# The gates of the last four chunks as one batch over 128 partitions

## The chip, the cores and the metric

The kernel runs on one core of a Trainium2 chip. The metric is the time of one execution on the device in microseconds (us), as the median of several runs. The engines are TensorE (PE: matmuls; PEld: loading of weights), VectorE (DVE), ScalarE (ACT), GpSimd (POOL) and SyncE (SP, which here only issues DMAs). Each works through its own queue in order.

## The reference

Two layers follow each other: a recurrent attention (mLSTM) with 4 batches, 8 heads, 768 steps and heads of 40, and a gated feed-forward layer on its output.

```python
for t in range(S):                                   # S = 768
    m_new = np.maximum(f_gate[:, :, t] + m, i_gate[:, :, t])
    f_stab = np.exp(f_gate[:, :, t] + m - m_new)
    i_stab = np.exp(i_gate[:, :, t] - m_new)
    m = m_new
    C = f_stab * C + i_stab * outer(vt, kt)          # per batch and head, 40 x 40
    n = f_stab * n + i_stab * kt
    y[:, :, t] = sigmoid(o_gate) * (C @ qt) / max(|n . qt|, 1)
# x: y with batch and step as rows (3072), head and channel as columns (320)
out = (sigmoid(x @ w_gate) * (x @ w_val)) @ w_out    # 320 -> 1536 -> 320
```

The change concerns only the running maximum `m` and the running sum of `f_gate`: two gates for each of 32 pairs (batch, head) and 768 steps.

## The kernel before

The steps are cut into 6 chunks of L = 128. A unit (c, b) is one chunk of one batch. Within a chunk the recurrence becomes matrix products: scores of q and k, times a matrix `d` of decay weights; between chunks a state `cst` is carried, scaled by `cdec`. The feed-forward layer works on chunk c for all four batches at once (512 columns), in 12 slices j of the 1536 hidden columns: `ffn_up` (L532 to L544) makes the two products into `pg0` and `pg1`, then `sg`, and its high and low parts `gh` and `gl`; `ffn_down` (L554 to L556) adds slice j into four banks `po`. The first four slices of chunk 0 are done in halves of 256 columns. Weights come as 64-bit numbers and are decoded piece by piece (`w_dec`: L259 on ScalarE, L264, L265, L269 on VectorE, L294 to L299 on ScalarE, L304 to L310 on POOL) between these slices.

The stages of a unit: `st_a` transposes q and k (L357) and copies them (L359, L361) and masks q (L362); `dmat` turns the loaded `d` tile into weights (L226 on ScalarE, mask L235 on POOL); `st_b` makes the scores (L426) and weights them (L427); `st_c` sums the values (L452), and with it the state is updated (`st_e`, L500 to L517) and the next unit's operands are prefetched (L135 to L138, `dmat_load` L219); `st_d` transposes the result into `xh` and `xl` (L488 to L491).

The gates. `f_gate` and `i_gate` are loaded as 32 rows (batch, head) by 768 steps into the tile `gin`, which holds the first slot of the tag "xh"; the running maxima lie in `mg`, the first slot of the tag "xl". Both slots are used again by `st_d` of chunk 1. Chunk 0 has its gates at the start (`gates_first`), chunk 1 in the opening (operation "gc"), chunks 2 to 5 in `gates_of(2, NCH)`: one running sum over 512 columns, which a tile `rst` of ones and zeros restarts at each chunk, one subtraction, then for each chunk a running maximum that starts at the end value `mend` of the chunk before, and the new end value; at last one subtraction of all maxima from the end values. Each chunk's maxima go to a scratch tensor `mscr[c]` in HBM, from which `dmat_load` reads them back, one row broadcast to all 128 partitions. `gate_transpose` (L195) turns sums and decays by TensorE, one transpose per chunk, into `at` (copied by VectorE, L197) and `dec` (exponential on ScalarE, L199), 128 steps by (chunk, batch, head); `gates_turn` derives `cdec` by a matmul (L207) and three VectorE operations (L208, L213).

The order outside the opening is a list of events by position, in units of a feed-forward slice, from a table `pos`, with clamps that keep it possible. A slice is emitted at its start, its `ffn_down` 0.46 later than the start of the slice behind it. The events g1, h1 and k1 stand for chunks 2 to 5's gates, `at` and `dec` with `cdec`; their positions are 0.599, 5.3 and 5.5. Position 4.0 is the first slice of 512 columns (its first matmul ends up on the queue at 76.6 us). The framework then makes each engine's queue from the emitted instructions by priority and its own model of what is ready when; `issue_after(x)` keeps instructions behind `x` on `x`'s engine.

Of the kernel before, what the change touches and what calls it, by code (L numbers as in the profile page):

```python
# [74 lines left out]
def mlstm_then_gated_ffn_kernel(  # L75
# [71 lines left out]
    mend = const.tile([BH, NCH + 1], F32, name="mend")  # L147
# [20 lines left out]
    def gate_max(c):  # L168
        cs = slice(c * L, (c + 1) * L)
        mc = m0[:BH] if c == 0 else mg[:, cs]  # L170
        nc.vector.tensor_tensor_scan(mc, ag[:, cs], ag[:, cs], mend[:, c : c + 1], ALU.max, ALU.max)
        nc.vector.tensor_tensor(mend[:, c + 1 : c + 2], fc[:, cs][:, L - 1 : L], mc[:, L - 1 : L], ALU.add)
        nc.sync.dma_start(mscr[c], mc)

    def gates_first():
        cs = slice(0, L)
        nc.vector.tensor_tensor_scan(fc[:, cs], ones, fg[:, cs], 0.0, ALU.mult, ALU.add)
        nc.vector.tensor_tensor(ag[:, cs], ig[:, cs], fc[:, cs], ALU.subtract)
        gate_max(0)


    def gates_of(c0, c1):
        cs = slice(c0 * L, c1 * L)
        nc.vector.tensor_tensor_scan(fc[:, cs], rst[:, cs.start - L : cs.stop - L], fg[:, cs], 0.0, ALU.mult, ALU.add)
        nc.vector.tensor_tensor(ag[:, cs], ig[:, cs], fc[:, cs], ALU.subtract)
        for c in range(c0, c1):
            gate_max(c)
        before = mend[:, c0:c1].unsqueeze(2).broadcast_to([BH, c1 - c0, L])
        nc.vector.tensor_tensor(dmx[:, cs].rearrange("p (c l) -> p c l", l=L), before,
                                mg[:, cs].rearrange("p (c l) -> p c l", l=L), ALU.subtract)  # L190

    def gate_transpose(src, dst, c0, c1, func):
        pt = ps_a.tile([P, c1 - c0, BH], F32, tag="pa", name=f"ptg{c0}_{c1}")
        for c in range(c0, c1):
            nc.tensor.transpose(pt[:, c - c0, :], src[:, c * L : (c + 1) * L], ident[:BH, :BH])  # L195
        if func is None:
            nc.vector.tensor_copy(dst[:, c0:c1, :], pt)  # L197
        else:
            nc.scalar.activation(dst[:, c0:c1, :], pt, func)  # L199
# [4 lines left out]
    def gates_turn(c0, c1):  # L204
        gate_transpose(dmx, dec, c0, c1, AF.Exp)
        pt = ps_a.tile([P, c1 - c0, B, H], F32, tag="pa", name=f"pt_cdec{c0}")
        nc.tensor.matmul(pt, sel, dec[:, c0:c1, :], start=True, stop=True)  # L207
# [8 lines left out]

    def dmat_load(c, b):
        d = dm_tile(c, b)
        nc.sync.dma_start(d, mscr[c][b * H : (b + 1) * H, :].partition_broadcast(P))  # L219
# [303 lines left out]
    def ffn_up(c, j, t0, t1):  # L523
# [20 lines left out]
        E('gl0' if c == 0 else 'gl').tensor_tensor(gl[u][:, :nt], sg, gh[u][:, :nt].bitcast(F32), ALU.subtract)  # L544
        return last
# [28 lines left out]
    def opening():  # L574
# [3 lines left out]
        nc.sync.dma_start(fg, f_gate.rearrange("b h s -> (b h) s"))  # L578
        nc.scalar.dma_start(ig, i_gate.rearrange("b h s -> (b h) s"))
# [28 lines left out]
        nc.gpsimd.memset(rst, 1.0)  # L608
        nc.gpsimd.memset(rst.rearrange("p (c l) -> p c l", l=L)[:, :, 0:1], 0.0)
# [333 lines left out]
```

## Time and profile before

| | |
|---|---|
| runs (median; lowest to highest of 3) | 572.35 us; 571.94 to 572.92 |
| span of the profiled execution | 569.9 us; the median of the runs is 2.45 us above it, and no separate time was kept for this execution |
| PE, PEld | 546.7 us (96%), 497.0 us (87%) |
| DVE, ACT, POOL | 319.5 us (56%), 232.2 us (41%), 162.2 us (28%) |
| DMA | 72.27 MB, mean 127 GB/s |

The profile is one execution. Times in it start at 0 with the span. The page gives for each engine the busy share in 40 slices of 14.25 us, and the chain of work that ended last; the timeline gives the single instructions, with start, duration, engine, line, output and inputs, and in brackets the time that the engine stood idle before it and what ended this. "ACT L299 ... [2.13 <-DVE dc L269]" reads: ScalarE idled 2.13 us before this instruction until VectorE's line 269, which writes dc, was done.

### The profile page before, as it was taken

To read this page: it belongs to the slowest core of one execution; us is meant where nothing else is said; L and a number is where in the kernel's file an instruction comes from. 1 tells how busy PE (TensorE), PEld (TensorE's weight loads), DVE (VectorE), ACT (ScalarE), POOL (GpSimd) and SP (SyncE) were. 2 spreads that over 40 slices of the span, in tenths; PEclk is the share of its full clock that TensorE was granted. 3 is DMA by queue.
4 is the path that set the end of the run, shared out by engine and by line. 5 is a ranking of instruction groups with operands and counts; after the bars stand their busy time and mean duration, and the time that the engine had idled before them with its cause. 6 is when DMAs were issued, how large, how long until landed. Compare 5 with 4: busy or idle time off the path is not lost.

```text
span 569.9 us, 9906 instructions
## 1 busy us (share of the span) xinstructions
PE 546.7 (96%) x3587; PEld 497.0 (87%) x3587; DVE 319.5 (56%) x739; ACT 232.2 (41%) x581; POOL 162.2 (28%) x231
## 2 busy tenths in 40 slices
PE   8667999999999999999999999999999999999997
PEld 7565988788899999998888888888888888999996
DVE  5788878895755645555555544545543545432322
ACT  5285657754443442352243241433342332232322
POOL 5567646575420241311322310332210210000000
PEclk9789999999999999999999999999999999999999
DMA  9797747242674947354666544685644824010000
GB/s 197 193 240 185 202 123 192 93 115 54 169 173 119 183 103 182 100 147 125 167 125 156 132 141 129 149 171 124 140 125 134 206 56 121 4 47 2 24 2 23
DMA packets 131641, 72.27 MB, mean 127 GB/s; under 512 B 103113, under 2 KB 120777, under 8 KB 131593
## 3 DMA queue, kind: packets, MB, share of 16 engines
q1 hardware_dynamic: 130504, 71.39, 50.6%
q8 instruction: 28, 0.46, 0.3%
q10 hardware_dynamic: 1088, 0.26, 0.2%
q14 instruction: 21, 0.16, 0.1%
HBM read 56.95 MB, written 14.68 MB: 126 GB/s over the span
## 4 chain that ended last, share of the span: by engine, by line
PE 85%; DVE 7%; ACT 3%; issue 2%; POOL 2%; POOLq 0%; DVEq 0%; ACTq 0%
PE pg L532 34%; PE po L554 7%; PE po L556 7%; PE po L555 7%; PE av L452 6%; PE pg L534 6%; PE pg L537 6%; PE in L447 2%; PE s L434 2%; PE pt L373 2%; PE xt L488 2%; PE cs L500 2%; PE s L426 1%; DVE dc L264 1%; ACT d L226 1%
## 5 line engine op out<-in xcount | busy, mean ns | idle before, releaser
L539 ACT ACTIVATE sg<-pg 128x256 f32<-128x256 f32 (+1 forms) x103 | 48.3, 469 | 174.3 <-PE pg L537 174.2
L540 DVE SCALAR_TENSOR_TENSOR sg<-sg,pg 128x256 f32<-128x256 f32 (+1 forms) x103 | 53.9, 524 | 113.9 <-ACT sg L539 110.6
L532 PE MATMUL pg<-xh,wl 128*128 128x256 f32 (+1 forms) x412 | 111.1, 342 | 1.2 <-POOL wl L304 1.2
L532 PE MATMUL pg<-xh,wh 128*128 128x256 f32 (+1 forms) x412 | 110.9, 343 | 0.4 <-DVE sg L540 0.4
L532 PE MATMUL pg<-xl,wh 128*128 128x256 f32 (+1 forms) x412 | 108.7, 339 | 0.0
L556 PE MATMUL po<-oh,gl 128*128 128x320 f32 x288 | 93.0, 323 | 0.0
L554 PE MATMUL po<-oh,gh 128*128 128x320 f32 x288 | 92.3, 321 | 0.4 <-ACT gh L543 0.4
L555 PE MATMUL po<-ol,gh 128*128 128x320 f32 x288 | 92.4, 321 | 0.0
L544 DVE TENSOR_TENSOR gl<-sg,gh 128x256 fp32r<-128x256 f32 (+1 forms) x103 | 59.6, 579 | 35.5 <-ACT gh L543 34.9
L532 PEld LDWEIGHTS pg<-xh,wl 128*128 128x128 f32 x412 | 70.9, 191 | 8.5 <-POOL wl L304 1.4
L532 PEld LDWEIGHTS pg<-xh,wh 128*128 128x128 f32 x412 | 70.9, 191 | 5.8 <-DVE sg L540 0.6
L532 PEld LDWEIGHTS pg<-xl,wh 128*128 128x128 f32 x412 | 69.3, 190 | 6.6
L543 ACT ACTIVATE gh<-sg 128x256 fp32r<-128x256 f32 (+1 forms) x103 | 51.7, 502 | 47.7 <-DVE sg L540 47.7
L554 PEld LDWEIGHTS po<-oh,gh 128*128 128x128 f32 x288 | 54.5, 189 | 2.0 <-ACT gh L543 0.6
L555 PEld LDWEIGHTS po<-ol,gh 128*128 128x128 f32 x288 | 54.4, 189 | 1.3
L556 PEld LDWEIGHTS po<-oh,gl 128*128 128x128 f32 x288 | 54.2, 188 | 0.5 <-DVE gl L544 0.2
L534 PE MATMUL pg<-xh,w 128*128 128x256 f32 (+1 forms) x206 | 52.9, 332 | 0.7 <-POOL v L139 0.4
L537 PE MATMUL pg<-xl,w 128*128 128x256 f32 (+1 forms) x206 | 53.1, 331 | 0.0
L452 PEld LDWEIGHTS av<-v,d 128*128 128x128 f32 x352 | 46.8, 191 | 2.2 <-DVE d L427 0.6
L452 PE MATMUL av<-v,d 128*128 128x41 f32 x352 | 45.5, 269 | 0.4 <-DVE d L427 0.3
L508 POOL TENSOR_TENSOR cst<-cst,cdec 120x246 f32<-120x246 f32 (+1 forms) x32 | 16.0, 519 | 98.9 <-PE in L447 98.9
L235 POOL TENSOR_SCALAR_AFFINE_SELECT d<-d 128x1024 f32<-128x1024 f32 x22 | 24.2, 1101 | 50.1 <-ACT d L230 46.0
(128 smaller groups left out, 834.5 us busy)
## 6 DMA issues: line engine op xcount, KB each, us to landing
d<-mscr SPq DMA_DIRECT2D x22, 512.0 KB
ks<-scr SPq DMA_DIRECT2D x16, 360.0 KB
qs<-scr SPq DMA_DIRECT2D x16, 360.0 KB
k<-in_k_dram SPq DMA_DIRECT2D x24, 160.0 KB
v<-in_v_dram SPq DMA_DIRECT2D x24, 160.0 KB
o<-in_o_gate_dram SPq DMA_DIRECT2D x24, 160.0 KB
st_o<-in_moe_w_out_dram SPq DMA_DIRECT2D x12, 320.0 KB
out_dram<-ob SPq DMA_DIRECT2D x24, 160.0 KB
```

Source lines behind the costliest of these rows:

```text
L235: nc.gpsimd.affine_select(out=d, in_=d, pattern=[[0, H], [1, L]], compare_op=ALU.is_ge, fill=0.0, base=0, channel_multiplier=-1)
L452: nc.tensor.matmul(pv[:, h, :], dm[u][:, h, :], vt[u][:, h, :], start=True, stop=True)
L532: nc.tensor.matmul(pg[n], w[n][:, a, fs], x[c][:, a, n0:n1], start=(i + a == 0), stop=False)
L534: nc.tensor.matmul(pg[n], w2[n][:, fs], xh[c][:, 2, n0:n1], start=False, stop=False)
L537: nc.tensor.matmul(pg[n], w2[n][:, fs], xl[c][:, 2, n0:n1], start=False, stop=True)
L539: nc.scalar.activation(sg, pg[0], AF.Tanh, scale=0.5)
L540: nc.vector.scalar_tensor_tensor(sg, sg, 1.0, pg[1], ALU.add, ALU.mult)
L543: last = nc.scalar.activation(gh[u][:, :nt], sg, AF.Copy)
L544: E('gl0' if c == 0 else 'gl').tensor_tensor(gl[u][:, :nt], sg, gh[u][:, :nt].bitcast(F32), ALU.subtract)
L554: nc.tensor.matmul(po[t], g1[:, ts], oh[:, j, :], start=(j == 0), stop=False)
L555: nc.tensor.matmul(po[t], g1[:, ts], ol[:, j, :], start=False, stop=False)
L556: nc.tensor.matmul(po[t], g0[:, ts], oh[:, j, :], start=False, stop=(j == NF - 1))
```

## The change

Only chunks 0 and 1 (NE = 2) keep the old form, on 32 partitions, and `gates_of` with its tile `rst` goes. Their loads are cut to 256 steps. The gates of chunks 2 to 5 are loaded by eight further DMAs onto 128 partitions, row (chunk, batch, head), 128 steps each. All four chunks then take one running sum, one subtraction and one running maximum of 128 columns (`late_sums`). What links the chunks is small: for each row the sum over its chunk and the end of its own maximum. These are spread into a 128 x 8 operand by the mask `mine` (which chunk a partition belongs to), and one matmul with `same` (ones where batch and head agree) brings the four chunks' values of a row to every partition of that row; a second matmul brings the end value of chunk 1. A scan of four columns chains them, each partition picks the value that its chunk starts from (`own`), and two operations finish maxima and decays (`late_chain`). The maxima go out by one DMA to one scratch tensor `mscl`. One transpose of 128 rows takes the place of four of 32. The event g1 moves from 0.599 to 4.6, and its VectorE instructions are queued behind the last `gl` emitted.

```diff
-... 'g1': 0.599, ...
+... 'g1': 4.6, ...
-    gin = two.tile([BH, 2, S], F32, tag="xh", name="gin")
+    NE = 2
+    NL = NCH - NE
+    gin = two.tile([P, 2 * NE * L + 2 * L], F32, tag="xh", name="gin")
...
+    def late_load():
+        for t, g in ((fl, f_gate), (il, i_gate)):
+            for c in range(NE, NCH):
+                p = (c - NE) * BH
+                nc.sync.dma_start(t[p : p + BH, :], g.rearrange("b h s -> (b h) s")[:, c * L : (c + 1) * L])
+
+    def late_sums():
+        one = tiny[:, 6, 0:1]
+        nc.vector.memset(one, 1.0)
+        nc.vector.tensor_reduce(mine, ident.rearrange("p (c m) -> p c m", m=BH), mybir.AxisListType.X, ALU.add)
+        nc.vector.tensor_reduce(fold, ident.rearrange("p (c m) -> p m c", m=BH), mybir.AxisListType.X, ALU.add)
+        nc.vector.tensor_copy(same.rearrange("p (c m) -> p c m", m=BH), fold.unsqueeze(1).broadcast_to([P, NL, BH]))
+        nc.vector.tensor_tensor_scan(fl, one.broadcast_to([P, L]), fl, 0.0, ALU.mult, ALU.add)
+        nc.vector.tensor_tensor(il, il, fl, ALU.subtract)
+        nc.vector.tensor_tensor_scan(ml, il, il, il[:, 0:1], ALU.max, ALU.max)
+
+    def late_chain():
+        ...
+        nc.vector.tensor_tensor(tot, fl[:, L - 1 : L], ml[:, L - 1 : L], ALU.add)
+        nc.vector.tensor_scalar(ends[:, :NL], mine, fl[:, L - 1 : L], None, ALU.mult)
+        nc.vector.tensor_scalar(ends[:, NL:], mine, tot, None, ALU.mult)
+        pe = ps_a.tile([P, 16], F32, tag="pa", name="ends")
+        nc.tensor.matmul(pe[:, : 2 * NL], same, ends, start=True, stop=True)
+        nc.tensor.matmul(pe[:, 2 * NL : 2 * NL + 1], same[:BH],
+                         mend[:, NE : NE + 1], start=True, stop=True)
+        nc.vector.tensor_copy(st[:, 0:1], pe[:, 2 * NL : 2 * NL + 1])
+        nc.vector.tensor_copy(ends, pe[:, : 2 * NL])
+        nc.vector.tensor_tensor_scan(st[:, 1:], ends[:, :NL], ends[:, NL:], st[:, 0:1], ALU.add, ALU.max)
+        nc.vector.tensor_tensor(pick, mine, st[:, :NL], ALU.mult)
+        nc.vector.tensor_reduce(own, pick, mybir.AxisListType.X, ALU.add)
+        nc.vector.tensor_scalar(fl, ml, own, own, ALU.max, ALU.subtract)
+        nc.vector.tensor_scalar(ml, ml, own, None, ALU.max)
+        nc.sync.dma_start(mscl, ml)
+
     def gate_transpose(src, dst, c0, c1, func, scale=1.0):
         pt = ps_a.tile([P, c1 - c0, BH], F32, tag="pa", name=f"ptg{c0}_{c1}")
-        for c in range(c0, c1):
-            nc.tensor.transpose(pt[:, c - c0, :], src[:, c * L : (c + 1) * L], ident[:BH, :BH])
+        n = src.shape[0]
+        nc.tensor.transpose(pt, src, ident[:n, :n])
...
-        nc.sync.dma_start(fg, f_gate.rearrange("b h s -> (b h) s"))
-        nc.scalar.dma_start(ig, i_gate.rearrange("b h s -> (b h) s"))
+        nc.sync.dma_start(fg, f_gate.rearrange("b h s -> (b h) s")[:, : NE * L])
+        nc.scalar.dma_start(ig, i_gate.rearrange("b h s -> (b h) s")[:, : NE * L])
...
-        nc.gpsimd.memset(rst, 1.0)
-        nc.gpsimd.memset(rst.rearrange("p (c l) -> p c l", l=L)[:, :, 0:1], 0.0)
...
             if kk == 0:
                 dmat_load(1, 0)
+                late_load()
             else:
-                gates_of(2, NCH)
+                with tc.issue_after(lastv.ins):
+                    late_sums()
+                    late_chain()
```

More of the change, by code (lines that the diff above doesn't have):

```diff
@@ L112, in mlstm_then_gated_ffn_kernel @@
     ps_a = ctx.enter_context(tc.tile_pool(name="ps_a", bufs=2, space=bass.MemoryType.PSUM))
-    gin = two.tile([BH, 2, S], F32, tag="xh", name="gin")
-    fg, ig = gin[:, 0, :], gin[:, 1, :]
-    mscr = [dram.tile([BH, L], F32, name=f"mscr{c}", tag=f"mscr{c}") for c in range(NCH)]
+    NE = 2
+    NL = NCH - NE
+    gin = two.tile([P, 2 * NE * L + 2 * L], F32, tag="xh", name="gin")
+    fg, ig = gin[:BH, : NE * L], gin[:BH, NE * L : 2 * NE * L]
+    fl, il = gin[:, 2 * NE * L :][:, :L], gin[:, 2 * NE * L + L :]
+    mscr = [dram.tile([BH, L], F32, name=f"mscr{c}", tag=f"mscr{c}") for c in range(NE)]
+    mscl = dram.tile([NL * BH, L], F32, name="mscl", tag="mscl")
     scr = [dram.tile([3, 2, D, 2, 3 * L], F32, name=f"scr{n}", tag=f"scr{n}") for n in range(2)]
@@ L145, in dm_tile @@
         return dm[(c, b)]
-    mend = const.tile([BH, NCH + 1], F32, name="mend")
+    mend = const.tile([BH, NE + 1], F32, name="mend")
     bmask = const.tile([P, 3, L], F32, name="bmask")
@@ L160, in mlstm_then_gated_ffn_kernel @@
     ident = const.tile([P, P], F32, name="ident")
-    mgr = two.tile([BH, 2, S], F32, tag="xl", name="mg")
-    mg, rst = mgr[:, 0, :], mgr[:, 1, L:]
+    mgr = two.tile([P, 5, L], F32, tag="xl", name="mg")
+    mg, ml = mgr[:BH, 0, :], mgr[:, 1, :]
+    same, fold = mgr[:, 2, :], mgr[:, 4, :BH]
+    tiny = mgr[:, 3, :].rearrange("p (n w) -> p n w", w=16)
+    mine = tiny[:, 0, :NL]
     fc, ag, dmx = fg, ig, fg
@@ L173, in gate_max, with gates_early @@
         nc.sync.dma_start(mscr[c], mc)
-    def gates_first():
-        cs = slice(0, L)
+    def gates_early(c):
+        cs = slice(c * L, (c + 1) * L)
         nc.vector.tensor_tensor_scan(fc[:, cs], ones, fg[:, cs], 0.0, ALU.mult, ALU.add)
         nc.vector.tensor_tensor(ag[:, cs], ig[:, cs], fc[:, cs], ALU.subtract)
[L179 to L185, printed above, removed]
-        for c in range(c0, c1):
[L187 to L190, printed above, removed]
@@ new lines, in late_chain @@
+    def late_chain():
+        ends, tot = tiny[:, 1, : 2 * NL], tiny[:, 2, 0:1]
+        st, own = tiny[:, 3, : NL + 1], tiny[:, 4, 0:1]
+        pick = tiny[:, 5, :NL]
+        nc.vector.tensor_tensor(tot, fl[:, L - 1 : L], ml[:, L - 1 : L], ALU.add)
[13 more added lines that the diff above has]
+        nc.sync.dma_start(mscl, ml)
@@ L193, in gate_transpose @@
+    def gate_transpose(src, dst, c0, c1, func, scale=1.0):
         pt = ps_a.tile([P, c1 - c0, BH], F32, tag="pa", name=f"ptg{c0}_{c1}")
-        for c in range(c0, c1):
-            nc.tensor.transpose(pt[:, c - c0, :], src[:, c * L : (c + 1) * L], ident[:BH, :BH])
+        n = src.shape[0]
+        nc.tensor.transpose(pt, src, ident[:n, :n])
         if func is None:
@@ L204, in gates_turn @@
     def gates_turn(c0, c1):
-        gate_transpose(dmx, dec, c0, c1, AF.Exp)
+        if c0 == NE:
+            gate_transpose(fl, dec, c0, c1, AF.Exp, scale=-1.0)
+        else:
+            gate_transpose(dmx[:, c0 * L : c1 * L], dec, c0, c1, AF.Exp)
         pt = ps_a.tile([P, c1 - c0, B, H], F32, tag="pa", name=f"pt_cdec{c0}")
@@ L857, in mlstm_then_gated_ffn_kernel @@
         ends[ins.engine] = ins
-    last = None
+    last = lastv = None
     def emit(p, kind, kk):
-        nonlocal last
+        nonlocal last, lastv
         c, b = divmod(kk, B)
         if kind == "up":
-            last = ffn_up(*tiles[kk])
+            last, lastv = ffn_up(*tiles[kk])
         elif kind == "down":
```

25 lines of the change are left out of this document (15 added, 10 removed), and 2 rows, old and new, of the table PARAM.

## The prediction

> **What bounds the kernel now.** I read the page's busy shares and slices first, then the chain, then the timelines of 28 to 45 us and of 84 to 106 us, where the moved work leaves and where it arrives.
>
> ```profile
> span 569.9 us, 9906 instructions
> PE   8667999999999999999999999999999999999997
> DVE  5788878895755645555555544545543545432322
> ```
>
> TensorE is full from the fifth slice (57 us) on, so what is to be gained lies in the first 55 us, and what is lost anywhere later is lost wholly. VectorE is busiest in slices 2 to 8, up to 114 us. The chain, in order of time, passes here through the gates of chunks 2 to 5:
>
> ```profile
> 29.18 1.67 DVE gin L184
> 30.87 1.05 DVE gin L185
> 31.95 1.35 DVE mg L171
> ```
>
> Who waits for it, from the timelines of ScalarE and TensorE (in brackets the idle time before, and what ended it):
>
> ```profile
> 31.71 1.10 ACT L259 ACTIVATE dc<-st_o 128x320 f32<-128x320 f32 x2
> 32.72 1.76 ACT L512 ACTIVATE cst<-cs,rmask 120x82 f32<-120x82 f32 x8
> 36.60 0.87 ACT L299 ACTIVATE oh<-dc 128x320 fp32r<-128x320 f32 x2 [2.13 <-DVE dc L269]
> 38.00 2.44 ACT L226 ACTIVATE d<-d,at 128x128 f32<-128x128 f32 x8
> 33.88 0.25 PE L195 MATMUL ptg<-ident,gin 32*128 32x32 f32 x1 [1.42 <-ACT cst L512]
> 37.13 0.33 PE L357 MATMUL pt<-ident,q 128*120 128x128 f32 x1 [3.00 <-DVE at L197]
> ```
>
> And two stretches, by windows (span and length, then busy time and count of PE, PEld, DVE, ACT and POOL, the granted clock, the DMA engines' share, GB/s):
>
> ```profile
> 34.40:37.80 3.40, 0.43 (x2) 0.19 (x2) 3.33 (x12) 1.27 (x6) 0.65 (x1) 0.96 0.96 232
> 37.80:41.20 3.40, 3.31 (x17) 3.28 (x18) 1.84 (x4) 3.40 (x12) 2.86 (x4) 0.54 0.99 203
> ```
>
> The weights' decoding (dc) was ready for VectorE at 32.81 and the transposed gate sums at 34.13; both stand behind the gates. ScalarE loses 2.13 us and TensorE 3.00 us. From 36.60 on ScalarE has no hole (busy 3.40 of 3.40 in the second stretch) while VectorE idles, so its 2.13 us is the price, not TensorE's 3.00.
>
> **The change part by part.** The gates of chunks 2 to 5, before:
>
> ```profile
> L184 DVE TENSOR_TENSOR_SCAN gin<-mg,gin x2: 401/1068/1734, 5.3 to 29.1; 32x128 f32<-32x128 f32 x1, 32x512 f32<-32x512 f32 x1
> L185 DVE TENSOR_TENSOR gin<-gin x2: 278/658/1039, 5.7 to 30.9; 32x128 f32<-32x128 f32 x1, 32x512 f32<-32x512 f32 x1
> L171 DVE TENSOR_TENSOR_SCAN mg<-gin,mend x5: 466/471/1345, 6.0 to 35.0; 32x128 f32<-32x128 f32 x5
> L172 DVE TENSOR_TENSOR mend<-gin,mg x5: 138/147/148, 6.5 to 37.0; 32x1 f32<-32x1 f32 x5
> L189 DVE TENSOR_TENSOR gin<-mend,mg x2: 280/833/1386, 6.7 to 37.2; 32x128 f32<-32x128 f32 x1, 32x512 f32<-32x512 f32 x1
> ```
>
> Of these chunks 2 to 5 have 1.73 + 1.04 + (1.35 + 3 x 0.47) + 4 x 0.15 + 1.39 = 7.5 us. They leave this place.
>
> *Removed wait.* ScalarE could follow L512 at 34.48 at once: up to 2.13 us. What is late next is the d tile of (0,3), which the L226 at 38.00 reads. It is 128 rows of 4096 bytes; the packets that start in three stretches:
>
> ```profile
> DMA packets 613, 0.52 MB, mean 258 GB/s; under 512 B 507, under 2 KB 507, under 8 KB 612
> DMA packets 962, 0.24 MB, mean 242 GB/s; under 512 B 939, under 2 KB 939, under 8 KB 962
> DMA packets 953, 0.15 MB, mean 149 GB/s; under 512 B 953, under 2 KB 953, under 8 KB 953
> ```
>
> In 34 to 36 us 105 large packets start, in 36 to 37 us 23, in 37 to 38 us none: 128, so the tile is there soon after 37, some 0.8 us before it is read. If ScalarE keeps its order, L226 gains 0.8 us; if L543 and L259 (gh, the next dc) are queued ahead of L226, they fill the hole and all 2.13 us come. I take 1.5, in the middle; ends 0.7 and 2.1.
>
> *Opening.* Two memsets of rst on POOL go, L608 the long one, and the two gate loads shrink from 96 KB each to 32 KB:
>
> ```profile
> 0.98 0.62 POOL L608 MEMSET mg<- 32x640 f32 x1
> 3.84 0.41 DVE L177 TENSOR_TENSOR_SCAN gin<-bmask,gin 32x128 f32<-32x128 f32 x1 [2.64 <-POOL bmask L156]
> 5.13 2.07 PE L643 MATMUL mb<-m,ident 128*128 128x128 f32 x8 [0.18 <-DVE m L171]
> 0.00:15.00 15.00, 13.08 (x70) 11.83 (x71) 8.59 (x22) 8.58 (x25) 8.28 (x29) 1.00 0.97 199
> ```
>
> The first scan waits for POOL's bmask, which comes 0.62 us earlier or a little more, and TensorE's first real work for that scan. The DMA engines are 97% busy in 0 to 15 us (the last two columns): 128 KB less at 199 GB/s is 0.64 us. Taken 0.4, since later operands hang on several queues; ends 0 and 0.7.
>
> *Late loads.* Eight DMAs of 16 KB stand on SP's queue behind the d tile of (1,0):
>
> ```profile
> 39.96 0.57 SPq L219 DMA_DIRECT2D d<-mscr  x1
> 45.10 0.38 SPq L277 DMA_DIRECT2D st<-in_moe_w_val_dram  x1
> ```
>
> Eight issues by 0.4 us are 3.2 us in a hole of 4.6: nothing, and if that cover goes, the L277 load is up to 1 us late. Four stores of mscr go from the queue, one comes.
>
> *The late place.* It stands behind the gl of the first tile of 512 columns, at 86.96:
>
> ```profile
> 84.58 0.47 PE L532 MATMUL pg<-xh,wh 128*128 128x512 f32 x1
> 86.96 0.68 DVE L544 TENSOR_TENSOR gl<-sg,gh 128x512 fp32r<-128x512 f32 x1
> 90.80 0.69 DVE L540 SCALAR_TENSOR_TENSOR sg<-sg,pg 128x512 f32<-128x512 f32 x1
> 95.36 0.63 PE L532 MATMUL pg<-xh,wh 128*128 128x512 f32 x2
> 98.80 0.67 DVE L540 SCALAR_TENSOR_TENSOR sg<-sg,pg 128x512 f32<-128x512 f32 x1
> 101.10 0.62 PE L532 MATMUL pg<-xh,wh 128*128 128x512 f32 x2
> 105.36 0.56 DVE L491 TENSOR_TENSOR xl<-xt,xh 128x384 fp32r<-128x384 f32 x1
> L178 DVE TENSOR_TENSOR gin<-gin x1: 278/278/278, 4.3 to 4.3; 32x128 f32<-32x128 f32 x1
> 96.06 0.38 PE L207 MATMUL pt_cdec<-dec,sel 128*128 128x128 f32 x2
> 87.60:105.00 17.40, 17.39 (x100) 14.92 (x100) 13.94 (x36) 14.50 (x42) 10.32 (x13) 1.00 0.58 145
> 105.00:125.00 20.00, 19.24 (x107) 16.31 (x106) 19.22 (x38) 11.92 (x27) 13.84 (x17) 1.00 0.40 116
> ```
>
> New VectorE work: two scans of 128 columns (0.47 each), six operations of 128 columns (two reductions, copy, subtraction, two tensor_scalar; 0.28 by L178) and nine small ones (0.15 by L172): 0.94 + 1.68 + 1.35 = 4.0 us. VectorE has 17.40 - 13.94 = 3.46 us free up to 105, and 0.78 in the next 20. So it is full there: work behind the gates comes 2 to 4 us later. TensorE's nearest need: the second half of the next tile at 95.36 needs the L540 of 90.80 to 91.49 (3.9 us of room), the one at 101.10 needs the L540 of 98.80 to 99.47 (1.6 us of room). That room takes most of it. I take 0.9 us lost; ends 0 (all in the room) and 3. TensorE's own work: eight transposes of 32 columns become two of 128, two small matmuls come, each in two passes like L207 (0.38): about +0.2 us, nearest to the small matmuls less what the fewer transposes save (ends -0.3, +0.8). The tiles gin and mg must be free for L491 at 105.36; the chain, even 4 us late, ends by about 96, and its one store has 9 us.
>
> Sum: -1.5 - 0.4 + 0.9 + 0.2 = -0.8 us on the profiled execution's span of 569.9, to 569.1. The runs' median is 572.35, 2.45 us more, which I take as unchanged: 571.5.
>
> *The clock behind TensorE's hole.* In the two stretches shown first TensorE is busy 0.43 of 3.4 us, and the granted clock in the next 3.4 us is 0.54. With the hole closed that stretch would run at full clock, 3.31 x 0.46 = 1.5 us less of TensorE. But ScalarE carries the chain there, so I give it nothing and make it part of a rival. [...]
>
> **The rivals.**
> - *More than forecast.* ScalarE's queue is filled by L543 and L259 (2.1), the opening gives 0.7, the clock's dip goes, and the late work fits: -2.8 to -3, 569.5. For: the rows above have room for each. Against: all must hold, and VectorE is full in 105 to 125.
> - *Given back.* VectorE's extra 4.0 us starve the weights' decoding (L264 to L269, which TensorE's next weights wait for) and TensorE loses the 1.9 again: 572.3. For: free time of 3.46 against 4.0. Against: the rooms of 3.9 and 1.6 us.
> - *Slower.* One place: the matmul of the chunk ends in TensorE's queue, which is in order. Its operand needs the late sums and the products, 2.2 + 0.45 us after 87.64, so about 90.3. TensorE is at the emission's place, ahead of the next up tile (the L532 of 84.58), at 84.6. Queued there it would stop TensorE 5.7 us; each us by which it is queued before 90.3 costs one, and from 1.9 on it decides. At 2 to 6 us the time is 572.5 to 576.5, likeliest about 574.3. For: the L357 at 37.13 stood 3.00 us behind a VectorE copy that came late just so. Against: the matmul L207, of the same kind, started at 96.06 with no wait ahead of it.
> - *It doesn't do what it says*: the d tile of (0,3) or another transfer is what ScalarE really stands on, and only 0.7 + 0 come, with 0.9 + 0.2 lost: 572.7; it ends like the second rival and shares its chance.
>
> **How the numbers follow.** Forecast (570.4 to 572.3): 0.50, of which 0.27 lies beyond -0.2%. More: 0.16. Given back or hidden: 0.17, of which 0.03 above +0.2%. Slower: 0.17. One in 500, 1.14 us, is about what a measurement can tell here: below 571.2 faster, 0.27 + 0.16 = 0.43; above 573.5 slower, 0.17 + 0.03 = 0.20; same 0.37. The range: 569.4 takes in nearly all of the first rival, 573.9 cuts the third near its middle; about 0.18 lies outside.
>
> **What would show it.** Right: no VectorE gate work in 28 to 38 us; L299 (oh) close behind L512, without the 2.13; the copy into at by 34.5 and L357 behind it; L226 of (0,3) starting near 37 with a DMA named as releaser, or L543 ahead of it; the clock at 1.0 around 38 to 41; the first scan near 3.2. Late: the chain between 87 and 96, TensorE's holes there under 1 us in sum. Wrong: a wait of TensorE of 2 us or more at the matmul of the ends or at the transposes behind it; SP's weight loads near 45 late by more than 2 us; L540 or the weights late so that up tiles at 101 or 105 wait; or the opening up to 28 us no earlier than before.

## The result and the profile after

The changed kernel takes 581.11 us (median of 4 runs, 578.19 to 584.15), the kernel before on the same chip 572.2: a ratio of 1.0141, 95% interval 1.0098 to 1.0184. It is slower by about 8 us by this ratio (8.9 us between the medians), where 0.8 us less was forecast. The profiled execution is the run of 584.15 us, the slowest of the four. First its span, the busy tenths and the granted clock in 40 slices of 14.56 us, from the page:

```profile
span 582.4 us, 9912 instructions
...
PE   8638998999899999999999999999999999999997
...
DVE  6539879896555565464565454555353545433322
...
PEclk9777999999789999999999999999999999999999
```

TensorE is no longer full from the fifth slice on (8 in slices 7 and 11), VectorE has 9 in slices 4, 7 and 9, and the clock is at 7 and 8 in slices 11 and 12 (146 to 175 us); before, it was at 9 from the fourth slice to the end. In the opening it stays low longer too (7 in slices 2 to 4, before 7, 8 and 9). Then the hole at 28 to 38 us. The gates are gone from it; what ScalarE waits for there, from 26 to 45 us, in the kernel before:

```profile
ACT xh L490 <- PE xt L488: 3.3, 1, 3.3
ACT oh L299 <- DVE dc L269: 2.1, 1, 2.1
```

and in the changed kernel:

```profile
ACT dc L302 <- DMA st_o<-in_moe_w_out_dram: 5.4, 1, 5.4
ACT d L269 <- DMA d<-mscr: 2.0, 1, 2.0
```

The 2.1 us behind the gates (oh) went, and two waits for DMAs stand in their place: a weight tile and the d tile of (0,3). SP's queue and ScalarE's timeline show them singly:

```profile
17.77 2.89 SPq L195 DMA_DIRECT2D gin<-in_f_gate_dram  x4
21.06 0.35 SPq L262 DMA_DIRECT2D d<-mscr  x1
...
27.12 1.85 SPq L195 DMA_DIRECT2D gin<-in_i_gate_dram  x4
...
34.77 0.79 SPq L262 DMA_DIRECT2D d<-mscr  x1
...
42.43 0.57 SPq L262 DMA_DIRECT2D d<-mscr  x1
```

```profile
34.27 0.48 ACT L302 ACTIVATE dc<-st_o 128x320 f32<-128x320 f32 x1 [5.36 <-DMA st_o<-in_moe_w_out_dram]
...
39.93 1.28 ACT L269 ACTIVATE d<-d,at 128x128 f32<-128x128 f32 x4 [2.05 <-DMA d<-mscr]
```

The eight late loads do not stand behind the d tile of (1,0), which is the one at 42.43: four are issued at 17.77, four at 27.12, ahead of the d tiles of (0,2) (21.06) and (0,3) (34.77). The first scan did come early (3.11 us, with bmask as releaser, where 3.84 stood).

Further on I follow the kernel by its up tiles, numbered in order of time (0 to 7 have 256 columns, 8 to 15 have 512, 16 begins chunk 1, 102 is the last), by the start of each tile's sg activation on ScalarE. The table gives it less that of the kernel before, in us, each from one profiled execution. Between two executions of one kernel the first three columns differ by 1.2 to 1.6 us (first two rows), so what counts is the growth from tile 3 to tile 102.

| kernel | 1 | 3 | 8 | 10 | 13 | 14 | 16 | 102 | growth |
|---|---|---|---|---|---|---|---|---|---|
| changed kernel | 2.0 | 2.5 | 3.0 | 5.3 | 5.0 | 7.3 | 7.1 | 12.5 | 9.9 |
| after_again | 0.3 | 1.3 | 1.8 | 4.1 | 3.9 | 6.1 | 5.5 | 5.5 | 4.2 |
| e1_hold_loads | -2.0 | -2.0 | -0.5 | 4.4 | 4.0 | 8.9 | 10.4 | 11.0 | 13.0 |
| e3_old_form_late | -0.6 | 0.4 | 0.8 | 3.4 | 2.7 | 5.2 | 4.6 | 4.7 | 4.2 |
| e4_rst_on_dve | -1.4 | -0.4 | -0.4 | -0.4 | -0.3 | -0.5 | -0.5 | -0.4 | 0.0 |
| e6_loads_first | 2.2 | 5.8 | 6.2 | 8.5 | 8.3 | 10.6 | 10.0 | 10.5 | 4.7 |
| e7_no_late_work | 0.7 | 0.7 | 2.1 | 3.8 | 4.5 | 6.7 | 6.1 | 6.5 | 5.8 |
| e8_place_26 | 0.5 | 1.2 | 6.3 | 7.2 | 9.8 | 13.2 | 13.0 | 14.2 | 13.1 |
| e9_new_form_old_place | 0.2 | -0.2 | 2.3 | 3.0 | 3.8 | 4.5 | 4.3 | 4.6 | 4.8 |
| e10_two_at_start | 0.7 | 0.7 | 1.2 | 3.5 | 3.3 | 5.6 | 5.0 | 5.4 | 4.7 |
| e11_two_no_work | 1.5 | 2.3 | 2.8 | 3.6 | 4.2 | 5.2 | 5.4 | 5.7 | 3.4 |
| e12_decode_ahead | 0.5 | 0.3 | 0.8 | 3.1 | 3.7 | 5.1 | 4.5 | 4.6 | 4.3 |
| e13_very_late | -2.3 | -1.3 | -0.9 | 0.1 | 1.5 | 2.2 | -1.5 | 5.8 | 7.1 |
| o1_no_work_old_order | 0.2 | 1.0 | 1.0 | 0.5 | 0.8 | 0.9 | 0.6 | 1.3 | 0.3 |
| o2_after_old_order | 1.2 | 1.5 | 1.5 | 5.9 | 6.0 | 6.0 | 6.0 | 6.1 | 4.7 |
| o3_before_new_order | 0.4 | 0.4 | 0.8 | 1.0 | 1.0 | 3.3 | 2.7 | 2.9 | 2.6 |
| o4_held_old_order | 0.7 | 1.6 | 1.6 | 4.8 | 5.0 | 5.1 | 4.8 | 5.2 | 3.6 |
| o5_place_26_old_order | -0.7 | -0.5 | 0.8 | 0.3 | 0.8 | 0.8 | 0.8 | 1.8 | 2.3 |
| o6_new_form_hole_old_order | 1.5 | 2.3 | 4.9 | 4.4 | 4.6 | 4.7 | 4.4 | 5.1 | 2.8 |

In the changed kernel three steps make the growth: 2.3 us from tile 8 to 10 (the late place), 2.3 from 13 to 14, and 5.5 from 16 to 17. With the 2.5 us of the opening they make nearly all of the 12.5 us between the two spans (582.4 and 569.9). What TensorE waits for between 84 and 140 us:

```profile
PE pg L575 <- ACT sg L582: 1.5, 3, 1.0
PE ends L216 <- DVE den L512: 0.9, 1, 0.9
PE s L469 <- DVE d L470: 0.7, 1, 0.7
PE cs L543 <- DVE t L492: 0.4, 1, 0.4
PE ptg L231 <- DVE qk L402: 0.3, 1, 0.3
```

Many waits, none of 2 us; the matmul of the ends has one of 0.9. The step at tile 14 in the timeline:

```profile
129.84 2.42 POOL L272 TENSOR_TENSOR d<-at,d 128x1024 f32<-128x1024 f32 x1 [0.20 <-DMA d<-mscl]
...
130.42 2.26 DVE L560 TENSOR_TENSOR cst<-cst,ct 120x246 f32<-120x246 f32 x2
132.61 0.48 DVE L312 SCALAR_TENSOR_TENSOR dc<-st_o,dc 128x320 int32<-128x320 int32 x1
133.12 0.47 ACT L342 ACTIVATE oh<-dc 128x320 fp32r<-128x320 f32 x1 [2.97 <-DVE dc L312]
...
133.86 0.58 ACT L582 ACTIVATE sg<-pg 128x512 f32<-128x512 f32 x1
```

The last step of a weight's decoding (L312) stands behind two state additions (L560); oh waits 2.97 us for it, and the tile's sg stands behind oh on ScalarE. In the kernel before, that decoding step stood ahead of the additions in VectorE's queue, and ahead of the gl that ran there beside POOL's addition into a d tile:

```profile
123.66 0.49 DVE L269 SCALAR_TENSOR_TENSOR dc<-st_o,dc 128x320 int32<-128x320 int32 x1
124.07 2.39 DVE L544 TENSOR_TENSOR gl<-sg,gh 128x512 fp32r<-128x512 f32 x1
126.38 1.24 DVE L517 TENSOR_TENSOR cst<-cst,ct 120x246 f32<-120x246 f32 x2
```

The step at tile 17 is the clock, by windows (span and length, TensorE's busy time and count, granted clock, DMA share, GB/s):

```profile
149.30:152.70 3.40, 1.91 (x9) 1.00 0.61 109
152.70:156.10 3.40, 3.13 (x15) 0.55 0.30 50
156.10:159.50 3.40, 3.40 (x19) 0.50 0.13 28
159.50:163.00 3.50, 3.50 (x16) 0.50 0.86 262
```

One window with TensorE busy 1.91 of 3.40 us, and then 10 us at half clock. This is not in every run: after_again, the same kernel run again, has clock 1.00 from 146 to 165 us and no step at tile 17. Of the eight runs of the two sets three have a mean clock of 0.973 or 0.974 and take 582.7 to 584.7 us, the other five 0.977 to 0.981 and 577.3 to 579.8; only one of each kind was profiled, so that the dip makes the difference in all three is likely and not shown.

### The profile page after: what moved, and what is told of

It reads as the page before. It is cut to its first block, busy times and chain, and to the rows that moved or that the text cites. A ratio compares the mean times of both kernels' runs of the same rounds, so it can differ in the third digit from the quotient of the medians.

```text
span 582.4 us, 9912 instructions
## 1 busy us (share of the span) xinstructions
PE 552.9 (95%) x3585; PEld 500.1 (86%) x3585; DVE 321.5 (55%) x745; ACT 232.1 (40%) x581; POOL 160.8 (28%) x229
## 3 DMA queue, kind: packets, MB, share of 16 engines
q1 hardware_dynamic: 130840, 71.45, 50.6%
## 4 chain that ended last, share of the span: by engine, by line
PE 82%; DVE 7%; ACT 4%; DMA 2%; POOL 2%; issue 2%; SPq 1%; POOLq 0%; DVEq 0%; ACTq 0%
PE pg L575 33%; PE po L597 7%; PE po L599 7%; PE po L598 7%; PE av L495 6%; PE pg L577 6%; PE pg L580 5%; PE in L490 3%; PE pt L416 2%; PE s L477 2%; PE cs L543 1%; PE xt L531 1%; PE s L469 1%; DVE dc L307 1%; DMA k<-in_k_dram 1%
## 5 line engine op out<-in xcount | busy, mean ns | idle before, releaser
L599 PE MATMUL po<-oh,gl 128*128 128x320 f32 x288 | 94.4, 328 | 0.4 <-DVE gl L587 0.4
L598 PE MATMUL po<-ol,gh 128*128 128x320 f32 x288 | 93.6, 325 | 0.0
L272 POOL TENSOR_TENSOR d<-at,d 128x1024 f32<-128x1024 f32 x16 | 31.5, 1967 | 28.9 <-DMA d<-mscl 25.5
```

The costliest lines, as they stand in the source:

```text
L272: E(arg).tensor_tensor(d, a, d, ALU.subtract)
L598: nc.tensor.matmul(po[t], g1[:, ts], ol[:, j, :], start=False, stop=False)
L599: nc.tensor.matmul(po[t], g0[:, ts], oh[:, j, :], start=False, stop=(j == NF - 1))
```

## The experiments

**Loads, place and opening.** T1 says here that the late loads make the loss in the opening, T2 that the late place makes all of it.

e1_hold_loads:

```diff
-                dmat_load(1, 0)
-                late_load()
+                d10 = dmat_load(1, 0)
+                with tc.issue_after(d10.ins):
+                    late_load()
```

> The changed kernel, with its eight late gate loads held on SP's queue until the load of the d tile of (1,0) is issued, as the prediction had assumed. T1 (the loads, issued at 17.8 and 27.1 us ahead of the d tiles of (0,2) and (0,3) and of two weight loads, delay the opening): the d tile of (0,3) lands near 37.4 again instead of 39.8, the second feed-forward tile's activation comes 0 to 1 us earlier than before the change instead of 1.96 later, and every later tile moves with it: about 2.8 us off the changed kernel's time, 576 to 578 where the clock dips near 153 us and 571 to 573 where it doesn't. T2 (the loads are hidden; the late place on VectorE and TensorE's in-order queue make all of the loss): the second tile stays 2 us late and the time near 581.

Measured: 585.78 us, ratio 1.0236 (1.0191 to 1.0282). The second tile came 2.0 us early (T1 said 0 to 1), and the time was worse than both theories have it: 1.8 us lost at tile 4, 4.8 from tile 9 to 10, 6.5 from 13 to 15. The last of these, 1.6 us from 14 to 15, falls into a stretch at clock 0.50 (134.6 to 141.5 us).

e3_old_form_late (in the kernel before):

```diff
-... 'g1': 0.599, ...
+... 'g1': 4.6, ...
-                gates_of(2, NCH)
+                with tc.issue_after(lastv.ins):
+                    gates_of(2, NCH)
```

> The kernel before, with the gates of chunks 2 to 5 in their old form (one scan of 512 columns on 32 partitions, four chained maxima, no matmul of the ends, no late loads), moved to the late place alone. T1: the opening gains up to 1 us by tile 1 since nothing is loaded late, the late place costs 2 to 3 us between 87 and 98 us (7.5 us of VectorE work instead of 4, so it can be 2 us more), no TensorE wait at a matmul of the ends: total 573 to 576. T2 (the matmul of the ends is what stops TensorE): no loss at the late place, total 570.5 to 572.

Measured: 576.05 us, 1.0051 (1.0024 to 1.0078). The late place costs with the old form too, and without any matmul of the ends; 2.4 us at tile 14 are there as well. With the gates out of the hole and no late load at all, the second tile is 0.6 us early and the fourth 0.4 us late; ScalarE has its 2 us of waiting in the hole again, now for the d tile of (0,3):

```profile
37.41 2.44 ACT L226 ACTIVATE d<-d,at 128x128 f32<-128x128 f32 x8 [2.25 <-DMA d<-mscr]
```

e4_rst_on_dve (in the kernel before):

```diff
-        nc.gpsimd.memset(rst, 1.0)
+        nc.vector.memset(rst, 1.0)
```

> The kernel before, with the two memsets of rst on VectorE instead of POOL and nothing else: the opening's part of the change alone. T1 (the opening's lead is lost at transfers that end when they did): the first scan near 3.2 instead of 3.84, TensorE's clock full some 3 us earlier, but the d tile of (0,2) lands when it did, the second feed-forward tile comes within 0.5 us of before and the time is 571.8 to 572.5. T2 (the lead is kept where nothing else delays it): the second tile 1 to 3 us earlier, time 569 to 571.

Measured: 571.93 us, 0.9995 (0.9972 to 1.0019). The time is T1's, its reason is not: the d tile of (0,3) landed 0.9 us earlier than before (last packet at 36.20, before 37.07) and the second tile came 1.4 us early, as T2 said; by the third only 0.4 us of this was left. The first scan came at 3.47 us, not 3.2, and what it waited for is now another thing, the gate's load:

```profile
3.47 0.47 DVE L177 TENSOR_TENSOR_SCAN gin<-bmask,gin 32x128 f32<-32x128 f32 x1 [1.49 <-DMA gin<-in_f_gate_dram]
```

e6_loads_first:

```diff
-                nc.sync.dma_start(t[p : p + BH, :], ...)
+                nc.scalar.dma_start(t[p : p + BH, :], ...)
         nc.scalar.dma_start(ig, ...)          # in opening()
+        late_load()
-                late_load()                   # behind the d tile of (1,0)
```

> The changed kernel, with the eight late gate loads issued on ScalarE's queue at the very start instead of on SP's. T1: the 128 KB are moved in the first 10 us, as before the change; SP's order for the d tiles and the weights is undisturbed, the d tile of (0,3) lands within 0.7 us of 37.4 and tile 1 comes within 1 us of before the change; the first q load on ScalarE's queue is up to 3 us later, which may take the opening's lead again. Total 577 to 579 with the clock dip, 572 to 574 without. T2: 581, tile 1 still 2 us late.

Measured: 580.57 us, 1.0132 (1.0083 to 1.0181). The time and the second tile (2.2 us late) are T2's; that tile 3 came 5.8 us late neither said. So the head of ScalarE's queue was no better place for the eight loads; how much of the step from tile 1 to 3 is their doing and how much TensorE's clock, at 0.50 from 47.9 to 61.5 us, is not told apart. The growth behind tile 3 is 4.7 us.

**Late work.** From here on T1 says that the late work's time on VectorE makes the late loss.

e7_no_late_work (e1 without it):

```diff
-                    late_sums()
-                    late_chain()
+                    nc.sync.dma_start(mscl, il)
```

> The changed kernel with the loads held behind the d tile of (1,0) as in the first experiment, and without the late work: sums, maxima, products, the matmuls of the ends and the scan of four columns are left out, the store takes the loaded gate as it is (so chunks 2 to 5 are computed from wrong sums); the two transposes and all that follows stay. T1 (the late work stands on VectorE ahead of the weights' decoding, in 88 to 128 us where VectorE is the bound, and makes all of the late loss): the loss of 4.8 us between tiles 9 and 10 and of 6.5 us between tiles 13 and 15 goes, tile 16 within 1 us of the kernel before, total 570.5 to 573. T2 (the loss comes from the rest of the changed order, transposes of 128 columns and the queues that moved): at least half of the loss stays, total 577 or more.

Measured: 578.64 us, 1.0124 (1.0089 to 1.0159). T1 fell: 5.8 us of growth with no late work at all, of which 1.8 come at tile 4, as in e1.

e8_place_26 (from e1):

```diff
-... 'g1': 4.6, ...
+... 'g1': 2.6, ...
```

> The changed kernel with the loads held, and the late work behind the gl of the second half of the chunk's second tile (some 70 to 75 us) instead of behind the first tile of 512 columns (88 us): VectorE had 3.5 us free of 15 in 60 to 75 and 1.9 of 13 in 75 to 88 us before the change. T1 (it is the place): the loss between tiles 9 and 15 falls from 10.5 to 2 to 5 us, of which 1 to 2 us come at tiles 6 to 8; total 573 to 578. T2 (VectorE's work up to 128 us is one queue, and 4 us more anywhere in it come out at tile 15): no change, 583 to 586.

Measured: 585.54 us, 1.0254 (1.0211 to 1.0297): no better than e1, as T2 said. 5.1 us of its growth come from tile 3 to 8, and two stretches of 3.4 us at clock 0.50 (from 70.6 and 118.3 us) lie in it.

e10_two_at_start, and e9_new_form_old_place (the same with `'g1': 0.599` and no `issue_after`):

```diff
-        for t, g in ((fl, f_gate), (il, i_gate)):
-            for c in range(NE, NCH):
-                ...
+        for t, g, eng in ((fl, f_gate, nc.sync), (il, i_gate, nc.scalar)):
+            eng.dma_start(t, g.rearrange("b h (c l) -> c (b h) l", l=L)[NE:])
```

> The changed kernel with the late gates loaded by two DMAs of 128 rows at the very start (one each on SP's and ScalarE's queue, behind the first gate loads) instead of eight on SP: the 128 KB move in the opening as in the kernel before. T1: no queue is disturbed by eight issues, d tiles as before, tiles 1 to 9 within 1 us of the kernel before or earlier; the late place costs what it cost, tile 15 6 to 10 us late, total 578 to 582. T2 (the late loads make most of the loss): total 572 to 575.

> The new form of the gates at the old place: two loads at the start as in the run with two at the start, and the sums, maxima and chain behind the opening (where the old form stood) instead of late. T1 (the place is what costs): some 2.5 us of VectorE work instead of 6 in the hole at 28 to 38 us, tile 1 0.5 to 2 us earlier than in the kernel before, no loss at tiles 9 to 15 beyond 1 us; total 569.5 to 572.5. T2 (the form costs, by its matmul and its small operations): 575 or more.

Measured: e10 577.24 us, 1.0106 (1.0069 to 1.0142), e9 579.65 us, 1.0159 (1.0108 to 1.021). In e10 the opening is within 0.8 us of before and the growth is 4.7: T1's way, with tile 15 5.0 us late where it said 6 to 10. e9 missed T1 and is T2's: at the old place too it grew by 4.8 us.

e11_two_no_work is e10 with the edit of e7, after_again the changed kernel itself. e12_decode_ahead (from e10) and the core of e13_very_late:

```diff
-... 'w29': 13.171, ...
+... 'w29': 8.73, ...
```

```diff
-... 'g1': 4.6, 'h1': 5.3, 'k1': 5.5, ...
+... 'g1': 12.55, 'h1': 12.8, 'k1': 12.95, ...
+        late = stage.tile([P, 6, L], F32, tag="st", name="late", bufs=3)
+    pos["l", 0] = 11.2                        # late_load, two DMAs on SP
```

> The run with two loads at the start, without the late work: sums, maxima, products, matmuls of the ends and the scan of four columns are left out and the store takes the loaded gate as it is (chunks 2 to 5 from wrong sums); transposes and the rest stay. The earlier run without late work still held eight loads on SP and lost 1.8 us at tile 4 by them. T1 (the late work takes VectorE's time from the weights' decoding): the decoding of out-weights 6, 7 and 11 comes ahead of the copy into at, the state additions and gl again, no loss from tile 8 to tile 16 (less than 1 us), total 571 to 573.5. T2 (the loss is not the late work's): 4 us from tile 8 to 16 as with it, total 576 to 578.

> The run with two loads at the start, with one number changed: the last weights' decoding is emitted at 8.73 instead of 11.99, ahead of the state additions of (1,1), so that VectorE's last decoding step of out-weight 11 stands ahead of these additions in its queue, as in the kernel before. T1 (the 2.3 us at tile 14 come from that step standing behind the additions, with ScalarE's oh behind it and the tile's sg behind oh): tile 14 loses 0 to 0.7 us on tile 13 instead of 2.3, total 575 to 576. T2 (VectorE is full there, whatever the order): tile 14 or 15 loses the same, total 577 to 578.

> The new form with buffers of its own, loaded by two DMAs some 140 us in, and the late work after the last weights are decoded (some 165 us), where VectorE had 3.2 of 8 us free; the d tiles of chunk 2 are loaded after it. T1 (the place is what costs): tiles 1 to 16 no later than in the kernel before, less the gates' hole and the loads in the opening, so 0.5 to 2.5 us earlier at tile 16, and no wait over 1 us at the ends' matmul; total 569.5 to 572. T2 (anything that moves the queues costs, or the matmul of the ends stops TensorE at any place): 574 or more.

> The changed kernel once more, on the same chip as these. T1: median 580 to 583, runs with and without the dip of TensorE's clock near 150 to 165 us, 5 us apart (576 to 579 and 581 to 585). T2 (no dip by chance, the same delay in each run): all runs within 1 us.

Measured: e11 577.93 us, 1.0095 (1.0068 to 1.0122); e12 579.8, 1.0113 (1.0074 to 1.0152); e13 579.11, 1.013 (1.0087 to 1.0173); after_again 579.12, 1.0129 (1.0071 to 1.0187), runs 577.26, 578.40, 579.84 and 584.71, with clocks 0.980, 0.979, 0.977 and 0.974: three runs together and one 5 us above them at the lowest clock, as T1 said, though the median lies below its 580. So e11 speaks against T1 once more (3.4 us of growth without the work). e12 gets back 0.8 of the 2.3 us at tile 14 and no time that can be told. e13 is 1.5 us early at tile 16, as T1 said, though tiles 11 to 15 were up to 2.2 us late on the way, and has 7.3 us lost behind it, so that the time is T2's; TensorE is busy 17.33 of 20 us at 165 to 185 us there (19.67 before), the rest I did not follow.

**Order.** All these kernels have in common that the instructions which the change does not touch stand in another order in the engines' queues, since the order is made anew for each program. T3 says that this makes the loss. So each instruction outside the opening (whose order is written by hand) was held behind its predecessor of the kernel before, on all five engines, with edges that fix the order and carry no data; in the traces of these runs TensorE, VectorE, ScalarE and POOL then work in that order from start to end, the gates aside:

```diff
+def order_as(tc, nc):
+    by = {i.name: i for i in nc.cur_bb.bb.instructions}
+    for seq in ORDER.values():          # numbers per engine, in the other kernel's order
+        for a, b in zip(seq, seq[1:]):
+            tc.add_manual_dep(by[f"I-{b}"], f"I-{a}", ...NoSync...)
```

o1 is e7 with two loads behind the d tile of (1,0), o4 the same with the late work, o2 the changed kernel, each in the order of before; o3 is the kernel before in the order of the changed one.

> Late gates loaded by two DMAs behind the d tile of (1,0), the late work left out (the store takes the loaded gate, chunks 2 to 5 from wrong sums), and on all five engines every other instruction held in the order of the kernel before. T3 (the order of the queues makes most of the loss from 80 to 145 us): no loss there, the opening's gain of 0.5 to 2 us kept, total 570 to 572. T1 (the order is not it): 575 or more, as in the two runs without late work.

> The changed kernel as it is, late work and eight loads on SP, with every other instruction held in the order of the kernel before on all five engines. T3: the 2.3 us at tile 14 go, and part of the loss of 2.1 to 2.8 us at tiles 9 and 10; the opening stays as in the changed kernel (0.3 to 2.5 us late at tile 3); total 574 to 577 without the clock dip near 153 us. T1: no gain by the order, 577 to 581, since VectorE's 4 us more come out at tile 15 in any order.

> The kernel before with nothing moved (gates of chunks 2 to 5 in the old form at the old place, no late loads), and every other instruction in the order of the changed kernel on all five engines. T3: it loses 2 to 4 us between tiles 8 and 15, total 574 to 576. T1: 572 to 573.

> As the first run of these four, with the late work in its place behind the gl of the first tile of 512 columns: the changed kernel with two late loads behind the d tile of (1,0) and the order of the kernel before. T3: the late work alone costs 0.5 to 2 us between tiles 8 and 15 and the opening gains 0.5 to 2: total 570.5 to 573.5. T1: 576 or more.

Measured: o1 572.73 us, 0.9997 (0.9967 to 1.0027); o2 578.53, 1.0119 (1.0092 to 1.0147); o3 574.3, 1.0036 (1.0021 to 1.005); o4 576.85, 1.009 (1.0058 to 1.0123). T3 holds for o1 and o3 behind the opening: without late work the time is 1.0095 in a new order (e11) and 0.9997 in the old one (o1; its two loads also stand elsewhere, and of the difference 3.1 us are growth behind tile 3), and the new order put into the kernel before, with nothing else changed, costs 2 us, 2.3 of growth at tile 14. T3's gain in the opening did not come in o1, whose time lies above the 570 to 572 it gave. The step at tile 14, now in o3, with a wait of oh of 2.97 us again:

```profile
125.54 2.06 POOL L229 TENSOR_TENSOR d<-at,d 128x1024 f32<-128x1024 f32 x1
...
125.77 2.39 DVE L544 TENSOR_TENSOR gl<-sg,gh 128x512 fp32r<-128x512 f32 x1
128.08 0.56 DVE L517 TENSOR_TENSOR cst<-cst,ct 120x246 f32<-120x246 f32 x2
128.56 0.48 DVE L269 SCALAR_TENSOR_TENSOR dc<-st_o,dc 128x320 int32<-128x320 int32 x1
129.07 0.47 ACT L299 ACTIVATE oh<-dc 128x320 fp32r<-128x320 f32 x1 [2.97 <-DVE dc L269]
...
129.81 0.58 ACT L539 ACTIVATE sg<-pg 128x512 f32<-128x512 f32 x1
```

The decoding step stands behind the gl this time, which ran beside POOL's addition for 2.39 us, and the two additions took 0.56. In both kernels the new order puts the step behind whatever VectorE does beside that POOL instruction (2.26 us of additions there, 2.39 us of gl here); in the old order it comes ahead of that.

For o2 and o4 T3's totals fall and T1's hold, though the step at tile 14 goes in both, as it said (6.0 and 6.0; 5.0 and 5.1): the late work has a price of its own, 0.9% (o4 against o1, intervals apart), 3.2 us of it from tile 8 to 10. In o2 4.4 us are lost there, with 3.4 us at clock 0.50 (97.0 to 100.4) among them. TensorE's waits of more than 0.3 us in o1, from 84 to 140 us:

```profile
PE s L467 <- DVE d L468: 1.0, 1, 1.0
```

and in o4:

```profile
PE pt L398 <- ACT ct L553: 1.3, 1, 1.3
PE s L467 <- DVE d L468: 1.0, 1, 1.0
PE pt L398 <- DVE at L231: 0.9, 1, 0.9
PE ends L214 <- DVE mg L212: 0.4, 1, 0.4
```

The way from the late work to ct, in o4's timeline:

```profile
89.20 0.28 DVE L198 TENSOR_REDUCE mg<-ident 128x4 f32<-128x128 f32 x1
...
90.49 0.48 DVE L203 TENSOR_TENSOR_SCAN mg<-gin 128x128 f32<-128x128 f32 x1
90.88 0.27 DVE L306 TENSOR_SCALAR dc<-dc 128x256 int32<-128x256 int32 x1
...
91.91 0.42 DVE L310 SCALAR_TENSOR_TENSOR dc<-st,dc 128x256 int32<-128x256 int32 x1
...
92.36 0.85 ACT L338 ACTIVATE w<-dc 64x256 fp32r<-64x256 f32 x2 [4.40 <-DVE dc L310]
...
94.89 1.11 ACT L553 ACTIVATE ct<-cs,rmask 120x82 f32<-120x82 f32 x5
...
96.05 0.32 PE L398 MATMUL pt<-ident,q 128*120 128x128 f32 x1 [1.35 <-ACT ct L553]
```

and the same two ScalarE instructions in o1:

```profile
89.89 0.86 ACT L338 ACTIVATE w<-dc 64x256 fp32r<-64x256 f32 x2 [2.52 <-DVE dc L310]
...
91.70 1.11 ACT L553 ACTIVATE ct<-cs,rmask 120x82 f32<-120x82 f32 x5
```

The decoding waits behind the late sums, ScalarE idles 4.40 us before the decoded weight where it idles 2.52 in o1, ct comes at 94.89 for 91.70 and TensorE's transposes behind ct. The late loads' own price is not told apart: o2 (eight on SP, early) against o4 (two, held) is 1.7 us by medians, with intervals that overlap.

o5 (o4 with `'g1': 2.6` for 4.6) and o6 (e9 in the order of before), where T4 says that the new form costs its time wherever it stands:

> As the run with held loads in the old order, with the late work behind the gl of the second tile of the chunk's second half (some 71 us in) instead of the gl of the first tile of 512 columns (some 88 us); all other instructions on all engines in the order of the kernel before. T3 (the price belongs to the place): VectorE was free 3.9 of 10 us in 70 to 80 us, so the 4 us fit but for 0 to 1 us; tiles 9 and 10 lose nothing; total 571 to 574. T4 (the new form costs 4 us of VectorE's work up to 128 us wherever it stands): tiles 6 to 10 lose 3 us, total 575.5 to 578.

> The new form of the gates at the old place (two loads at the start, late sums behind the opening; the matmul of the ends and the chain come out near 55 us in VectorE's queue), all other instructions in the order of the kernel before. T3: VectorE's work in the hole at 28 to 38 us is 3 us shorter than in the old form, which gains nothing since nothing was gained by taking it out wholly; the chain at 55 us costs 0 to 1 us; total 571.5 to 573.5. T4: 575 or more.

Measured: o5 573.37 us, 1.0025 (0.9998 to 1.0051); o6 577.44, 1.0078 (1.005 to 1.0106). o5 is T3: with the same 5.1 us of work at 71 us, where VectorE had room, tile 7 loses 1.3 us and tiles 8 to 10 nothing, and the time cannot be told from before. VectorE's third figure in windows of the kernel before:

```profile
70.00:80.00 10.00, 10.00 (x67) 9.08 (x66) 6.13 (x18) 5.94 (x14) 4.06 (x4) 1.00 0.50 161
80.00:90.00 10.00, 9.67 (x58) 8.30 (x57) 9.56 (x23) 4.48 (x10) 5.70 (x6) 1.00 0.57 182
```

3.87 us free in the first ten, 0.44 in the second. e8 is the same place without the order, and with eight loads for two: 585.5. o6 missed T3, and its time is T4's: 2 us lost at tile 4, near its chain, and 2.3 in the opening, where the d tile of (0,3) landed 2.1 us later than before (last packet at 39.14); why it did is open. No version beat the kernel before; o1, which leaves work out, only equals it.

## Why the prediction was wrong

Two terms of the sum failed: the removed wait (-1.5), which had at most 0.4 us to give, and the late place (+0.9), which cost 3 to 5. Two things had no term: the order of the other instructions, and a clock that fell near 153 us.

*Removed wait, -1.5: failed; some 0.4 us at most were there to gain, and the time shows nothing.* The wait for the gates did go. In o1 the gates are out of the hole, the opening is that of the changed kernel and only two loads are added; oh starts at 34.48 instead of 36.60, just where the prediction put it. What was to follow did not:

```profile
34.48 0.85 ACT L340 ACTIVATE oh<-dc 128x320 fp32r<-128x320 f32 x2
...
38.20 2.45 ACT L267 ACTIVATE d<-d,at 128x128 f32<-128x128 f32 x8 [2.24 <-DMA d<-mscr]
```

The activation of the d tile of (0,3) waits 2.24 us for its DMA and starts 0.2 us later than the 38.00 of before. I had this tile ready 0.8 us before it was read, from the start of its last packet, and took 1.5 as the middle between that and the whole 2.13, which needed ScalarE to do other work ahead of this activation; neither in o1 nor in the changed kernel does it. By the traces its last packet ends at 37.07 in the kernel before and at 37.62 in o1, whose load was issued 0.45 us later. In each of the 19 other profiled executions the activation starts 0.4 to 0.6 us behind that packet's end and the second tile's sg 5.4 to 5.6 us behind it, whatever VectorE does in the hole; in the kernel before it was 0.9 and 5.9. So the second tile follows the landing of this tile, and the gates held it back by some 0.4 us at most, not 1.5. The time of o1 (0.9997) alone would not settle it: 1.9 us for this step and the next would be 0.9967, the end of the interval, and 1.5 us 0.9974, inside it. The weight tile st_o, for which ScalarE waits 3.67 us until 32.47 in o1, costs nothing there, since oh was on time. The rival that the change doesn't do what it says had this mechanism.

*Opening, -0.4: not contradicted, not shown.* Scan and bmask came as said. e4's tiles are 0.4 us early from tile 2 to the end, less than two executions of one kernel differ by there, and 0.4 us cannot be told in its time (0.9995).

*Late loads, 0: the premise failed, the price is open.* "Eight DMAs stand on SP's queue behind the d tile of (1,0)": I took the place of emission for the place in the queue. They were issued 15 and 25 us ahead of it. The last packet of the d tile of (0,3) then ended at 37.9 to 39.5 us (three executions: the changed kernel, after_again, o2), and at 35.5 to 38.1 us in the six with held loads; the ranges overlap.

*Late place, +0.9 (0 to 3): 3 to 5 us (o4 against o1: 3.3 us of growth, 4.1 between the medians, 0.9% by ratio).* The work, the sum of its 17 operations on VectorE, is 4.8 us in the changed kernel and 5.1 in o5, for 4.0 estimated; the sum that failed is the room. I took it from two L540 (3.9 and 1.6 us) and not from the decoding, oh and ct, which stand right behind the late sums; ct came 3.2 us later. The rival "given back" named the decoding and priced it at 1.9.

*Order: no term at all.* The prediction had every other instruction keep its place. The order is worth 2 us in the kernel before (o3) and some 5 without late work (e11 against o1, which differ in the place of two loads as well; 3.1 us of it behind the opening); with the late work it cannot be told (after_again 1.0129, o2 1.0119).

*The slower rival* had another mechanism: the matmul of the ends waited 0.9 us (0.4 in o4), not 2 to 6, since it was queued near its operand.

*The clock* after the hole was given nothing, and the hole did stay: in o1 TensorE idles 4.00 us up to 34.02, before 1.42 and 3.00. The half clock even grew, to 32.8 to 39.6 and 43.0 to 49.8 us in o1 and 33.6 to 40.4 and 43.8 to 50.6 in the changed kernel, where it was 37.5 to 40.9 before. Time goes with it: in the nine executions in which the half clock ends within 5 us of the second tile's sg or ahead of it, the way to the fourth tile takes 20.0 to 20.7 us (before 20.4); in the other eleven, where it lasts longer, 21.0 to 21.5 (o1 21.2) and once 24.1 (e6). No experiment changes the clock alone, so that it is the cause is argued. The full clock that the prediction gave to a closed hole was an estimate from two stretches; o1 and the changed kernel do not show it, since the hole is open in both (in the changed kernel TensorE idles 6.95 us up to 35.82). That the clock could dip near 153 us I had not seen. With that dip the growth is 9.9 us and without it 4.2.

## What to carry to other kernels

Before a stall is priced, ask of each transfer under it when it lands, also of those that nobody waits for yet, and count from the end of its last packet to the start of its reader: here 2.13 us of waiting went, and a wait of 2.24 us for a transfer stood in its place. Work that is moved must fit at its new place by what stands right behind it in each queue, and the room is to be read there, in short windows (10 us here), not from the two consumers that come to mind. Where a program's order is made anew for each build, compare the queues first, and test a change with the old order held: here a kernel without the late work stood at 1.0095 in one order and at 0.9997 in the other.

## What the runs showed of the hardware

In the changed kernel TensorE's clock fell to 0.5 for 10 us (0.55, 0.50 and 0.50 in the three windows from 152.70 to 163.00 us) after one window in which it was busy 1.91 of 3.40 us, 56%; its longest single idle time there was 0.92 us (up to 152.97). In the three windows at the low clock TensorE was busy 3.13, 3.40 and 3.50 us, and the clock came back behind them (0.96 from 163.00 to 166.40 us). What set off the fall is not shown.

The two state additions L560 took 2.26 us beside POOL's L272 in the changed kernel and 0.56 in o3, where no POOL work ran beside them; the gl of o3 took 2.39 us beside the same POOL addition (L229 there), the next gl, 6 us later, 0.69. What makes the difference is not shown.
